# Softmax denominators of a sliding-window attention: from TensorE matmuls to a ones column in V and a VectorE partition shuffle, with TensorE tile modes batched by the scheduler

## The chip, the cores and the metric

One core of a Trainium2 chip. The time is the device time of one execution in microseconds (us). Ratios are computed as the mean time of one kernel's fast runs over that of the other's of the same rounds on the same chip, so they are not quite the ratio of the medians that are quoted beside them. The experiments ran on four occasions, whose medians of the kernel before were 432.86, 433.57, 433.21 and 433.63 us; compare times across occasions by their ratios.

## The reference, cut to what matters

Four layers over x of 2048 tokens by 448 channels, in bf16: attention, gated MLP, attention, gated MLP, each after a layer norm and with a residual. The attention has 16 heads of 28 channels, and every query sees 8 keys at distances 0, 2, ..., 14:

```python
x = x + _A_ref(_layernorm(x, axis=-1), A_wqkv, A_wo)            # layer 0
x = x + _B_ref(_layernorm(x, axis=-1), B_w_gate, B_w_up, B_w_down)  # layer 1
x = x + _A_ref(_layernorm(x, axis=-1), A_wqkv, A_wo)            # layer 2
x = x + _B_ref(_layernorm(x, axis=-1), B_w_gate, B_w_up, B_w_down)  # layer 3
# in _A_ref:  logits = einsum(q, kg) * scale; attn = softmax(logits); o = einsum(attn, vg)
```

## The kernel before

The program is a list of operations with estimated durations, which a list scheduler puts in a fixed order for each engine when the kernel is built; at run time the engines follow that order and wait for each other by semaphores. It works on even and odd tokens separately, so that the dilated window becomes a dense band, in blocks of up to 120 queries (36 blocks in the two attention layers). One block is: 16 score matmuls (TensorE in row tiles, four heads side by side), Exp on ScalarE (ACT), a mask multiply on VectorE (DVE) or GpSimd (POOL), then this, which is where the change is:

```python
def attn_back(li, qb, slot, prio):
    bk = Banks(2)                              # two PSUM banks (PSUM: the memory that TensorE writes; 8 banks)
    for b in range(4):                         # denominators: ones^T E, on 32 rows each
        E.matmul(ps[32*b:32*b+32, bk[1], 0:4*nq], ones32[0:nk, :], E_sb[0:nk, slot, b, 0:4*nq], tile_position=(0, 32*b))
    for h in range(H):                         # attention times V, in column tiles
        b, hc = h % 4, h // 4
        E.matmul(ps[32*b:32*b+32, bk[0], hc*nq:hc*nq+nq], v_sb[0:nk, vs, DH*h:DH*h+32], E_sb[0:nk, slot, b, hc*nq:hc*nq+nq], tile_position=(0, 32*b))
    # ACT: R = exp(-ln(denominator));  DVE: oT = ps * R
    ... (cut)
```

oT then goes through the output projection `wo_g` (operation Y), is added to x, and through the next layer norm. The channel count of 448 is three and a half times 128, so most products end in a "tail" of 64 rows; two tails share the array in 64-row tiles. So TensorE has four modes: full (F), 64-row tiles (R64), 32-row tiles for the scores (R32), 32-column tiles for attention times V (C32). The rule by which the scheduler picks an operation for TensorE was simply: the ready one of the highest priority that gets its banks.

```python
cands.sort()                 # by priority
for *_, op in cands:
    ... (bank checks, cut)
    best = op
    break
```

The softmax here doesn't subtract the row's maximum and nothing guards it: scores larger than these inputs give would overflow.

Of the kernel before, what the change touches and what calls it, by code (L numbers as in the profile page):

```python
# [4 lines left out]
ACT = mybir.ActivationFunctionType  # L5
# [3 lines left out]
D = 448  # L9
# [18 lines left out]
TAILS = True  # L28
PE_T = ("00", "01")
HEAD_LN = 4  # L30
POOL_MASK = 2
POOL_WQK = True
LN0 = (1, 1, 2)
# [18 lines left out]

class Op:
    __slots__ = ("engs", "ins", "est", "deps", "mode", "prio", "acquire", "release", "idx", "eng",
                 "dma", "lat", "after", "start", "end", "promise", "cls")

    def __init__(self, **kw):
        for k in self.__slots__:
# [11 lines left out]
class Sched:  # L70
# [74 lines left out]
    def schedule(self):  # L145
        self.holder = [None] * 8
        self.free_at = [-1e9] * 8
        self.last_rel = [None] * 8
        free = {e: 0.0 for e in self.ENGS}
        order = {e: [] for e in self.ENGS}  # L150
        mode = None
        open_promise = 0
        ndep, users = {}, {}
        pend = {e: [] for e in self.ENGS}
        self.dgroup = {}
        for op in self.ops:
            if op.dma is not None:
                self.dgroup.setdefault((op.dma, op.mode), []).append(op)
        for op in self.ops:
            srcs = set()  # L160
            for k in op.deps:
                src = self.ready[k][0]
                srcs |= {src.idx} if src.dma is None else {o.idx for o in self.dgroup[(src.dma, src.mode)]}
            if op.after is not None:
                srcs.add(op.after.idx)
            ndep[op.idx] = len(srcs)
            for s in srcs:
                users.setdefault(s, []).append(op)
            if not srcs:
                for e in op.engs:  # L170
                    pend[e].append(op)
        left = len(self.ops)
        now = 0.0
        while left:
            moved = False
            b_ready = any(o.acquire is not None and o.acquire.kind == 1 for o in pend["pe"])
            for e in self.ENGS:
                if free[e] > now + 1e-6:
                    continue
                best = None  # L180
                cands = []
                for op in pend[e]:
                    r = self.ready_at(op, e)
                    if r <= now + 1e-6:
                        cands.append((op.prio if e == "pe" or not FIFO else op.cls, r if e != "pe" and FIFO else 0, op.idx, op))
                cands.sort()
                a_wait = False
                for *_, op in cands:
                    if op.acquire is not None:
                        if op.promise > 0 and open_promise:  # L190
                            continue
                        held = [0, 0]
                        for h in self.holder:
                            if h is not None:
                                held[h.kind] += 1
                        kind = op.acquire.kind
                        cap = (A_CAP if b_ready else 8) if kind == 0 else (B_CAP if a_wait else 8)
                        if op.promise >= 0 and held[kind] + op.acquire.n + (op.promise * 2) > cap:
                            continue
                        if self.pick_banks(op.acquire, now) is None:  # L200
                            if kind == 0:
                                a_wait = True
                            continue
                    best = op
                    break
                if best is None:
                    continue
                op = best
                op.eng = e
                for x in op.engs:  # L210
                    pend[x].remove(op)
                if op.acquire is not None:
                    op.acquire.b = self.pick_banks(op.acquire, now)
                    for b in op.acquire.b:
                        self.holder[b] = op.acquire
                        if self.last_rel[b] is not None:
                            op.deps.append(self.last_rel[b])
                open_promise += op.promise
                est = op.est[e]
                if e == "pe":  # L220
                    if mode is not None and op.mode != mode:
                        est += self.SWITCH
                    mode = op.mode
                op.start, op.end = now, now + est
                free[e] = op.end
                order[e].append(op)
                for bk, i in op.release:
                    b = bk.b[i]
                    assert self.holder[b] is bk
                    self.holder[b] = None  # L230
                    self.free_at[b] = op.end + self.TAIL[op.eng]
                    key = ("rel", op.idx, b)
                    self.ready[key] = (op, len(op.ins) - 1)
                    self.last_rel[b] = key
                left -= 1
                moved = True
                for u in users.get(op.idx, ()):
                    ndep[u.idx] -= 1
                    if ndep[u.idx] == 0:
                        for x in u.engs:  # L240
                            pend[x].append(u)
            if moved:
                continue
            nxt = None
            for e in self.ENGS:
                if not pend[e]:
                    continue
                if free[e] > now + 1e-6:
                    c = [free[e]]
                else:  # L250
                    c = [self.ready_at(op, e) for op in pend[e]]
                    c += [f + self.LAT for f in self.free_at]
                c = [t for t in c if t > now + 1e-6]
                if c and (nxt is None or min(c) < nxt):
                    nxt = min(c)
            assert nxt is not None, "stuck"
            now = nxt
        self.order = order
        self.total = max(op.end + op.lat for op in self.ops)
# [77 lines left out]
def build(nc, A_x, A_wqkv, A_wo, B_w_gate, B_w_up, B_w_down, out):  # L337
# [46 lines left out]
    def one(fn, key=None):  # L384
        return [(fn, key)]
# [28 lines left out]
    sc.add("pool", one(lambda E: E.memset(WQK[:].rearrange("p c w (h e) -> p (c w h) e", e=32)[:, :, DH:32], 0.0), "c_wqk0"), 700, prio=-45)  # L414
    memset("pool", xnT[0][:, :, 0:PAD], 0.0, "c_p0", 150)
    memset("pool", xnT[0][:, :, SEG:SEG + PAD], 0.0, "c_p1", 150)
    memset("pool", v_sb[:, :, D:D + 32], 0.0, "c_v", 200)
    memset("pool", qk[:, :, :, 0:PAD], 0.0, "c_p2", 200)
    memset("pool", qk[:, :, :, SEG:SEG + PAD], 0.0, "c_p3", 200)
    memset("pool", MK[:], 1.0, "i_mk0", 300)  # L420
# [174 lines left out]
    def v_group(li, qbs, prio):  # L595
# [31 lines left out]
        s0 = slots[0][0]  # L627
        nk = infos[0][4]
        def fn(E):
            dst = v_sb[0:nk, s0:s0 + n, 0:D]  # L630
            src = ps[0:nk, bk[0]:bk[0] + n, 0:D]
            return E.activation(dst, src, ACT.Copy) if hasattr(E, "activation") else E.tensor_copy(dst, src)  # L632
        sc.add(("act", "dve"), one(fn, [("V", li, q) for q in qbs]), {"act": act_est(n * D), "dve": dve_est(n * D)},
               deps=list(keys) + [p for _, p in slots] + ["c_v"], release=[(bk, 0), (bk, 1)], prio=prio)
# [3 lines left out]
    def attn_front(li, qb, prio):  # L638
# [5 lines left out]
        deps = [("QK", li, j, c) for j in range(jl, jh + 1) for c in range(4)]  # L644
        slot, prev = ring("e", ("AV", li, qb))
        bk = Banks(4, pair=True)
        ins = []
        for h in range(H):
            b, hc = h % 4, h // 4
# [17 lines left out]

    def attn_back(li, qb, slot, prio):
        r, k, t0, nq, nk, tok = qb_info(qb)
        bk = Banks(2)  # L670
        vs = vslot[(li, qb)]
        ins = []
        for b in range(4):
            ins.append((lambda E, b=b: E.matmul(ps[32 * b:32 * b + 32, bk[1], 0:4 * nq], ones32[0:nk, :], E_sb[0:nk, slot, b, 0:4 * nq], start=True, stop=True, tile_position=(0, 32 * b)),  # L674
                        ("Dn", li, qb) if b == 3 else None))
        for h in range(H):
            b, hc = h % 4, h // 4
            ins.append((lambda E, b=b, hc=hc, h=h: E.matmul(ps[32 * b:32 * b + 32, bk[0], hc * nq:hc * nq + nq], v_sb[0:nk, vs, DH * h:DH * h + 32],  # L678
                                                            E_sb[0:nk, slot, b, hc * nq:hc * nq + nq], start=True, stop=True, tile_position=(0, 32 * b)),
                        ("AV", li, qb) if h == H - 1 else None))  # L680
        sc.add("pe", ins, 200.0 + 4 * 54.0, deps=[("E", li, qb, 0), ("E", li, qb, 1), ("V", li, qb), "c_ones"], mode="C32", acquire=bk, prio=prio)
        rs, prev = ring("r", ("N", li, qb))
        sc.add("act", one(lambda E: E.activation(R_sb[:, rs, 0:4 * nq], ps[:, bk[1], 0:4 * nq], ACT.Ln), ("Rl", li, qb)), act_est(4 * nq),  # L683
               deps=[("Dn", li, qb), prev], release=[(bk, 1)], prio=prio)
        sc.add("act", one(lambda E: E.activation(R_sb[:, rs, 0:4 * nq], R_sb[:, rs, 0:4 * nq], ACT.Exp, scale=-1.0), ("R", li, qb)), act_est(4 * nq, False),  # L685
               deps=[("Rl", li, qb)], prio=prio)
        war = [("Y", li - 2, B) for B in range(tok // 128, (tok + nq - 1) // 128 + 1)] if li >= 2 else []
# [190 lines left out]
```

## Time and profile before

432.74 us (median of 3 runs, 432.32 to 433.1). First the page's line of busy times.

```profile
span 431.5 us, 7732 instructions
...
PE 412.2 (96%) x3180; PEld 173.9 (40%) x3220; DVE 244.3 (57%) x482; ACT 221.3 (51%) x350; POOL 24.7 (6%) x38
```

TensorE (PE) is the busiest by far. Whether it is the limit everywhere is read from the windows (busy us of each engine in a stretch, with the number of instructions; the last three columns are granted clock, DMA share and GB/s):

```profile
core 0: us, PE busy (x) PEld busy (x) DVE busy (x) ACT busy (x) POOL busy (x), PEclk, DMA share, GB/s
20.00:40.00 20.00, 17.08 (x208) 7.21 (x208) 11.15 (x23) 17.07 (x25) 6.42 (x3) 1.00 0.74 196
40.00:60.00 20.00, 16.76 (x204) 7.26 (x195) 18.05 (x35) 14.34 (x22) 4.01 (x2) 1.00 0.29 47
...
100.00:150.00 50.00, 49.42 (x438) 20.96 (x435) 32.87 (x71) 30.00 (x47) 0.00 (x0) 1.00 0.17 33
...
250.00:300.00 50.00, 49.58 (x374) 20.72 (x378) 26.97 (x51) 27.04 (x40) 0.00 (x0) 1.00 0.06 12
```

From 100 to 400 us TensorE has about 1% of air (time in which it runs nothing). In the two windows from 20 to 60 us it has 15%, while ACT (17.07 us in the first) or DVE (18.05 us in the second) is as full as it is or fuller. The time up to the first gate matmul of layer 1 is called the head below. Its first record is at 62.52 us; the weight loads around it (62.27, 62.30 and 62.52 us) show that one record is missing, so the head of the kernel before ended some 0.2 us earlier.

"Busy" of TensorE is wide, because matmuls overlap; what a matmul costs is how far it moves the start of the next. That is read from the timeline (start, length, engine, line, shape, how many were merged; an idle gap would stand in brackets):

```profile
104.25 1.49 PE L758 MATMUL ps<-WD,hT 128*128 128x448 bf16 x7
105.67 0.39 PE L650 MATMUL ps<-qk 28*128 28x120 bf16 x16
105.99 1.50 PE L758 MATMUL ps<-WD,hT 128*128 128x448 bf16 x7
...
109.17 0.39 PE L674 MATMUL ps<-E_sb,ones 128*32 128x480 bf16 x4
109.38 0.38 PE L678 MATMUL ps<-E_sb,v_sb 128*32 128x120 bf16 x16
109.69 1.19 PE L551 MATMUL ps<-WV,xnTa 128*72 128x448 bf16 x4
```

Seven matmuls of 448 columns take 105.67 - 104.25 = 1.42 us. Inside a row they follow each other in 189 ns, so 7 x 189 = 1.32 us, and the missing 0.1 us is the step into another tile mode. The four ones matmuls take 109.38 - 109.17 = 0.21 us. Over all records of the trace after 65 us the medians are 189 ns between full matmuls of 448 columns and 283 to 285 ns when a tiled one follows; 216 ns for 512 columns and 309 to 312 ns before a tiled one; 308 ns from the last tail into full mode. A change of mode costs about 94 ns, whichever way it goes.

The groups of the operations in question, from the list by shape (busy us, mean ns of one, idle time before them and what ended it):

```profile
L689 DVE TENSOR_TENSOR oT<-ps,R_sb 128x480 bf16<-128x480 f32 x32 | 20.8, 651 | 12.3 <-ACT R_sb L685 10.6 <-PE ps L551 1.6
...
L674 PE MATMUL ps<-E_sb,ones 128*32 128x480 bf16 x128 | 12.4, 376 | 1.4 <-POOL E_sb L663 1.4
...
L586 DVE CAST qk<-ps 128x1024 bf16<-128x1024 f32 x3 | 3.7, 1222 | 0.9 <-PE ps L524 0.9
```

### The profile page before, as it was taken

What the parts mean: (1) busy time and instruction counts of PE and PEld (TensorE: products, weight loads), DVE (VectorE), ACT (ScalarE), POOL (GpSimd) and SP (SyncE); (2) the same over time, 40 slices, a digit from 0 to 9 for tenths busy, and PEclk for the clock granted to TensorE, in tenths of its full rate; (3) what the DMA queues carried; (4) which work ended last, traced back from release to release, by engine and by line L of the source; (5) the groups of instructions that cost most, each with busy time, mean ns of one, the idle gap of its engine ahead of it and who ended that gap; (6) DMA issues with size and microseconds to landing.
All of it is one profiled execution on the core that took longest, in us unless ns stands there. A gap on an engine that the chain in (4) does not pass through costs nothing.

```text
span 431.5 us, 7732 instructions
## 1 busy us (share of the span) xinstructions
PE 412.2 (96%) x3180; PEld 173.9 (40%) x3220; DVE 244.3 (57%) x482; ACT 221.3 (51%) x350; POOL 24.7 (6%) x38
## 2 busy tenths in 40 slices
PE   6897799999999999999999999999999999999997
PEld 4333334444443345334453334433444344344333
DVE  5746967465896278514887148822876432442332
ACT  4679766756565673347643565346853321321330
POOL 3715210000000000000000000000000000000000
PEclk9999999999999999999999999999999999999999
DMA  8794130100031200200202200010022101001001
GB/s 283 223 277 75 26 50 14 38 0 2 2 74 30 45 2 2 49 2 1 50 2 61 38 2 2 14 38 0 14 59 47 24 11 33 0 2 43 0 2 43
DMA packets 37220, 18.11 MB, mean 42 GB/s; under 512 B 31137, under 2 KB 36273, under 8 KB 37185
## 3 DMA queue, kind: packets, MB, share of 16 engines
q1 hardware_dynamic: 34880, 11.02, 11.7%
q0 software_dynamic: 1152, 5.22, 4.1%
q10 hardware_dynamic: 1152, 1.38, 1.0%
q8 instruction: 25, 0.41, 0.4%
q14 instruction: 11, 0.08, 0.1%
HBM read 8.43 MB, written 1.84 MB: 24 GB/s over the span
## 4 chain that ended last, share of the span: by engine, by line
PE 87%; ACT 5%; issue 4%; DMA 2%; DVE 1%; POOLq 0%; POOL 0%; SPq 0%; DVEq 0%
PE ps L512 47%; PE ps L758 20%; PE ps L524 9%; PE ps L703 5%; ACT E_sb L657 2%; PE ps L674 2%; PE ps L650 2%; DMA x_sb<-in_A_x_dram 2%; PE ps L678 1%; PE ps L551 1%; ACT R_sb L683 1%; ACT qk L586 0%; POOLq L831 0%; POOL E_sb L663 0%; ACT R_sb L685 0%
## 5 line engine op out<-in xcount | busy, mean ns | idle before, releaser
L746 DVE TENSOR_TENSOR hT<-g_sb,ps 128x512 bf16<-128x512 bf16 x112 | 75.9, 685 | 94.2 <-ACT g_sb L743 69.9
L743 ACT ACTIVATE g_sb<-ps 128x512 bf16<-128x512 f32 x112 | 65.7, 598 | 93.0 <-PE ps L524 78.8
L758 PE MATMUL ps<-WD,hT 128*128 128x448 bf16 x448 | 91.0, 353 | 0.0
L512 PE MATMUL ps<-xnTb,WU 128*128 128x512 bf16 x327 | 89.5, 379 | 1.1 <-issue 0.6
L512 PE MATMUL ps<-xnTb,WG 128*128 128x512 bf16 x313 | 86.4, 380 | 2.9 <-issue 1.4
L657 ACT ACTIVATE E_sb<-ps 128x960 bf16<-128x960 f32 (+1 forms) x72 | 63.3, 926 | 29.8 <-PE ps L650 29.8
L708 DVE TENSOR_TENSOR x_sb<-x_sb,ps 128x448 bf16<-128x448 bf16 x64 | 39.2, 613 | 34.0 <-PE ps L758 25.5
L663 DVE TENSOR_TENSOR E_sb<-E_sb,MK 128x960 bf16<-128x960 bf16 (+1 forms) x66 | 41.0, 625 | 29.8 <-ACT E_sb L657 29.4
L758 PEld LDWEIGHTS ps<-WD,hT 128*128 128x128 bf16 x448 | 42.1, 98 | 39.1
L512 PE MATMUL ps<-xnTa,WQK 128*128 128x512 bf16 x184 | 46.6, 390 | 3.0 <-ACT WQK L434 1.6
L512 PEld LDWEIGHTS ps<-xnTb,WU 128*128 128x128 bf16 x336 | 32.1, 98 | 38.4 <-issue 0.6
L512 PEld LDWEIGHTS ps<-xnTb,WG 128*128 128x128 bf16 x336 | 26.4, 97 | 50.2 <-issue 29.2
L473 DVE BATCH_NORM_STATS2 st<-x_sb 128x6 f32<-128x448 bf16 x64 | 39.1, 618 | 4.1 <-DMA x_sb<-in_A_x_dram 3.2
L586 ACT ACTIVATE qk<-ps 128x1024 bf16<-128x1024 f32 x29 | 29.7, 1024 | 20.1 <-PE ps L524 13.8
L524 PE MATMUL ps<-xnTb,WT 64*128 64x512 bf16 x224 | 33.9, 381 | 0.0
L683 ACT ACTIVATE R_sb<-ps 128x480 f32<-128x480 f32 (+1 forms) x36 | 19.7, 550 | 22.0 <-PE ps L674 22.0
L689 DVE TENSOR_TENSOR oT<-ps,R_sb 128x480 bf16<-128x480 f32 (+1 forms) x36 | 22.4, 625 | 14.2 <-ACT R_sb L685 12.4
L703 PE MATMUL ps<-wo_g,oT 128*128 128x448 bf16 x128 | 28.9, 353 | 1.1 <-DVE oT L689 1.0
L512 PEld LDWEIGHTS ps<-xnTa,WQK 128*128 128x128 bf16 x192 | 17.0, 99 | 28.4 <-issue 9.2
L484 DVE TENSOR_SCALAR xn_sb<-x_sb,mv,rstd 128x512 bf16<-128x512 bf16 x64 | 23.5, 426 | 2.8 <-ACT rstd L478 2.7
L512 PE MATMUL ps<-WV,xnTa 128*128 128x448 bf16 x96 | 21.4, 353 | 0.9 <-ACT E_sb L657 0.8
L632 ACT ACTIVATE v_sb<-ps 128x896 bf16<-128x896 f32 (+1 forms) x17 | 14.8, 873 | 13.5 <-PE ps L524 13.1
(55 smaller groups left out, 210.8 us busy)
## 6 DMA issues: line engine op xcount, KB each, us to landing
x_sb<-in_A_x_dram SPq DMA_DIRECT2D x4, 448.0 KB, 7.8
out_dram<-x_sb SPq DMA_DIRECT2D x16, 112.0 KB, 1.7
WD<-in_B_w_down_dram POOLq DMA_DIRECT2D x1, 1568.0 KB, 14.4
WG<-in_B_w_gate_dram POOLq DMA_DIRECT2D x3, 448.0 KB, 5.0
WU<-in_B_w_up_dram POOLq DMA_DIRECT2D x3, 448.0 KB, 7.9
hT<-in_A_wqkv_dram ACTq DMA_DIRECT2D x4, 224.0 KB, 5.1
xnTb<-xn_sb SPq DMA_TRANSPOSE x32, 2.5
WV<-in_A_wqkv_dram ACTq DMA_DIRECT2D x4, 112.0 KB, 6.1
```

The lines of the kernel that those rows point to most:

```text
L473: sc.add("dve", one(lambda E, B=B: E.bn_stats(st6[:, B, :], x_sb[:, B, :]), ("bn", li, B)), 525.0, deps=[("x", li - 1, B)] + ([("xn", li - ...
L512: ins.append((lambda E, u=u, c=c, st=st, sp_=sp_, which=which: E.matmul(u["out"](which), u["lhs"](which, c, 0, 128), u["rhs"](which, c, 0, ...
L524: ins.append((lambda E, u=u, c=c, lo=lo, which=which, opening=opening: E.matmul(u["out"](which), u["lhs"](which, c, lo, lo + 64), u["rhs"] ...
L586: return E.activation(dst, src, ACT.Copy) if hasattr(E, "activation") else E.tensor_copy(dst, src)
L657: return E.activation(E_sb[0:nk, slot, 2 * hp:2 * hp + 2, 0:4 * nq], ps[0:nk, b0:b0 + 2, 0:4 * nq], ACT.Exp, scale=SCALE)
L663: return E.tensor_tensor(e, e, m, ALU.mult)
L683: sc.add("act", one(lambda E: E.activation(R_sb[:, rs, 0:4 * nq], ps[:, bk[1], 0:4 * nq], ACT.Ln), ("Rl", li, qb)), act_est(4 * nq), deps= ...
L703: ins.append((lambda E, hc=hc: E.matmul(ps[:, bk[0], 0:D], oT[:, hc, lo:hi], wo_g[:, hc, :], start=hc == 0, stop=hc == 3), ("Y", li, B) if ...
L708: sc.add("dve", one(lambda E: E.tensor_tensor(x_sb[:, B, :], x_sb[:, B, :], ps[:, bk[0], 0:D], ALU.add), ("x", li, B)), dve_est(D), deps=[ ...
L743: sc.add("act", one(lambda E, gs=gs, bk=bk: E.activation(g_sb[:, gs, :], ps[:, bk[0], :], ACT.Copy), ("G", li, j, fc)), act_est(512), deps ...
L746: sc.add("dve", one(lambda E, gs=gs, bk=bk, fc=fc: E.tensor_tensor(hT[:, fc, hs, :], g_sb[:, gs, :], ps[:, bk[1], :], ALU.mult), ("H", li, ...
L758: ins.append((lambda E, fc=fc, bk=bk, i=i: E.matmul(ps[:, bk[0], 0:D], hT[:, fc, hs, 128 * i:128 * i + 128], WD[:, fc, :], start=fc == 0, ...
```

## The change

Two things. (1) V gets a stride of 32 columns per head instead of 28, and the four spare columns hold ones. The attention matmul is 32 columns wide anyway, so row 28 of each group of 32 PSUM rows now holds the denominator at no extra TensorE work; a DVE shuffle copies that row to all 32 rows, and Ln, Exp and the multiply go on as before. Only the first four blocks (`D_PE = 1`) keep the ones matmuls. (2) When TensorE is in full mode, the scheduler holds tiled operations back until two are ready (`HOLD_N`) or one has waited long enough; once in a tiled mode, it takes all ready tiled operations before it returns.

```diff
-    memset("pool", v_sb[:, :, D:D + 32], 0.0, "c_v", 200)
+    sc.add("pool", one(lambda E: E.memset(v_sb[:]...[:, :, DH:32], 1.0), "c_v"), 400, prio=-40)
@@ scheduler
-                    best = op
-                    break
+                    okay.append(op)
+                    if e != "pe":
+                        break
+                if okay and e == "pe":
+                    nf = [op for op in okay if op.mode != "F"]
+                    ff = [op for op in okay if op.mode == "F"]
+                    if mode not in (None, "F"):
+                        same = [op for op in nf if op.mode == mode]
+                        best = (same or nf or ff)[0]
+                    elif not nf or not ff:
+                        best = okay[0]
+                    else:
+                        over = [now - op.seen >= ((HOLD_BA if op.prio < -5 else HOLD_BB) if b_ready else HOLD_A) for op in nf]
+                        if len(nf) >= HOLD_N or any(over):
+                            best = nf[0]
+                        else:
+                            best = ff[0]
@@ attn_front: an order between blocks
+        if (li > 0 or jh >= S_AFTER) and qb % NQP:
+            deps = deps + [("E", li, qb - 1, 0), ("E", li, qb - 1, 1)]
@@ attn_back
+        by_pe = li == 0 and (tok + nq - 1) // 512 < D_PE
+        bk = Banks(2 if by_pe else 1)
         for b in range(4):
+            if not by_pe:
+                break
             ins.append(... ones matmul ...)
-            ... v_sb[0:nk, vs, DH * h:DH * h + 32] ...
+            ... v_sb[0:nk, vs, 32 * h:32 * h + 32] ...
+            sc.add("dve", one(lambda E: E.stream_shuffle(R_sb[:, rs, 0:4 * nq], ps[:, bk[0], 0:4 * nq], [DH] * 32), ("Rs", li, qb)), dve_est(4 * nq) + 100.0, ...)
+            sc.add("act", one(lambda E: E.activation(R_sb[...], R_sb[...], ACT.Ln), ("Rl", li, qb)), ...)
```

(Cut: constants, the write of V with the new stride, the estimates, most of the lines that these replace, and the old path, which stays for blocks with `by_pe`.)

More of the change, by code (lines that the diff above doesn't have):

```diff
@@ L30 @@
 HEAD_LN = 4
+HOLD_A = 1000.0
+HOLD_BA = 3000.0
+HOLD_BB = 0.0
+HOLD_N = 2
+D_PE = 1
+S_AFTER = 2
 POOL_MASK = 2
@@ L54 @@
     __slots__ = ("engs", "ins", "est", "deps", "mode", "prio", "acquire", "release", "idx", "eng",
-                 "dma", "lat", "after", "start", "end", "promise", "cls")
+                 "dma", "lat", "after", "start", "end", "promise", "cls", "seen")
     def __init__(self, **kw):
@@ L187, in schedule @@
                 a_wait = False
+                okay = []
                 for *_, op in cands:
@@ L203, in schedule @@
                             continue
-                    best = op
-                    break
+                    okay.append(op)
+                    if e != "pe":
+                        break
+                hold = None
+                if okay and e == "pe":
+                    for op in okay:
+                        if op.seen is None:
+                            op.seen = now
+                    nf = [op for op in okay if op.mode != "F"]
[11 more added lines that the diff above has]
+                            best = ff[0]
+                elif okay:
+                    best = okay[0]
                 if best is None:
@@ L416, in build @@
     memset("pool", xnT[0][:, :, SEG:SEG + PAD], 0.0, "c_p1", 150)
-    memset("pool", v_sb[:, :, D:D + 32], 0.0, "c_v", 200)
+    sc.add("pool", one(lambda E: E.memset(v_sb[:].rearrange("p s (h e) -> p (s h) e", e=32)[:, :, DH:32], 1.0), "c_v"), 400, prio=-40)
     memset("pool", qk[:, :, :, 0:PAD], 0.0, "c_p2", 200)
@@ L629, in fn @@
         def fn(E):
-            dst = v_sb[0:nk, s0:s0 + n, 0:D]
-            src = ps[0:nk, bk[0]:bk[0] + n, 0:D]
+            dst = v_sb[0:nk, s0:s0 + n, :].rearrange("p s (h e) -> p s h e", e=32)[:, :, :, 0:DH]
+            src = ps[0:nk, bk[0]:bk[0] + n, 0:D].rearrange("p s (h e) -> p s h e", e=DH)
             return E.activation(dst, src, ACT.Copy) if hasattr(E, "activation") else E.tensor_copy(dst, src)
@@ L669, in attn_back @@
         r, k, t0, nq, nk, tok = qb_info(qb)
-        bk = Banks(2)
+        by_pe = li == 0 and (tok + nq - 1) // 512 < D_PE
+        bk = Banks(2 if by_pe else 1)
         vs = vslot[(li, qb)]
@@ L677, in attn_back @@
             b, hc = h % 4, h // 4
-            ins.append((lambda E, b=b, hc=hc, h=h: E.matmul(ps[32 * b:32 * b + 32, bk[0], hc * nq:hc * nq + nq], v_sb[0:nk, vs, DH * h:DH * h + 32],
+            ins.append((lambda E, b=b, hc=hc, h=h: E.matmul(ps[32 * b:32 * b + 32, bk[0], hc * nq:hc * nq + nq], v_sb[0:nk, vs, 32 * h:32 * h + 32],
                                                             E_sb[0:nk, slot, b, hc * nq:hc * nq + nq], start=True, stop=True, tile_position=(0, 32 * b)),
                         ("AV", li, qb) if h == H - 1 else None))
-        sc.add("pe", ins, 200.0 + 4 * 54.0, deps=[("E", li, qb, 0), ("E", li, qb, 1), ("V", li, qb), "c_ones"], mode="C32", acquire=bk, prio=prio)
+        sc.add("pe", ins, (200.0 if by_pe else 0.0) + 4 * 54.0, deps=[("E", li, qb, 0), ("E", li, qb, 1), ("V", li, qb), "c_ones", "c_v"], mode="C32", acquire=bk, prio=prio)
         rs, prev = ring("r", ("N", li, qb))
-        sc.add("act", one(lambda E: E.activation(R_sb[:, rs, 0:4 * nq], ps[:, bk[1], 0:4 * nq], ACT.Ln), ("Rl", li, qb)), act_est(4 * nq),
-               deps=[("Dn", li, qb), prev], release=[(bk, 1)], prio=prio)
+        if by_pe:
+            sc.add("act", one(lambda E: E.activation(R_sb[:, rs, 0:4 * nq], ps[:, bk[1], 0:4 * nq], ACT.Ln), ("Rl", li, qb)), act_est(4 * nq),
+                   deps=[("Dn", li, qb), prev], release=[(bk, 1)], prio=prio)
+        else:
+            sc.add("dve", one(lambda E: E.stream_shuffle(R_sb[:, rs, 0:4 * nq], ps[:, bk[0], 0:4 * nq], [DH] * 32), ("Rs", li, qb)), dve_est(4 * nq) + 100.0,
+                   deps=[("AV", li, qb), prev], prio=prio)
+            sc.add("act", one(lambda E: E.activation(R_sb[:, rs, 0:4 * nq], R_sb[:, rs, 0:4 * nq], ACT.Ln), ("Rl", li, qb)), act_est(4 * nq, False),
+                   deps=[("Rs", li, qb)], prio=prio)
         sc.add("act", one(lambda E: E.activation(R_sb[:, rs, 0:4 * nq], R_sb[:, rs, 0:4 * nq], ACT.Exp, scale=-1.0), ("R", li, qb)), act_est(4 * nq, False),
```

## The prediction

> **What bounds it.** TensorE. The page: PE 412.2 of 431.5 us busy (96%), DVE 57%, ACT 51%, clock at full throughout. In the timeline its matmuls start back to back. In windows, PE is busy 49.4 to 49.8 of every 50 us from 100 to 400 us. The exception is the head, up to the first gate matmul at 62.5 us: in 20-40 us and 40-60 us PE is busy 17.1 and 16.8 of 20 us, while ACT (17.1) or DVE (18.1) is fuller.
>
> **What the change does, costed from the timeline.**
> 1. Ones matmuls. The four 128x480 ones matmuls of a query block push the next group back 0.21 us (109.17 to 109.38); the short block costs 0.12 us. They stay for the first 4 blocks and go for 32: 28 x 0.213 + 4 x 0.12 = 6.4 us of PE. V columns stay 32 wide, so the ones column is free for PE.
> 2. Tile modes. A WD matmul advances PE 189 ns, but 283 ns when a tiled group follows; 128x512 goes 216 to 312 ns into row tiles, tails 216 to 308 ns out of them, and a direct step between two tiled modes costs the same. So about 94 ns per change. The Trainium skill, "TensorEngine Tiling (Array Packing)", Key Properties, says a mode change drains TensorE; the trace agrees, with 94 ns. By the instruction orders, changes go from 290 to 252: 38 x 94 ns = 3.6 us (head 40 to 44, rest 250 to 208).
> 3. Added to DVE: 32 shuffles of 128x480 f32 from PSUM. The same-size PSUM multiply into oT takes 0.65 us; I estimate 0.6 to 0.65 us each, near 20 us in all (57% to about 63%). ACT keeps its count; Ln only reads SBUF instead of PSUM. The attention tail gets one more hop, about 0.7 us, plus deliberate holding.
>
> **On the critical path.** After the head, all PE savings count: 5.8 us of ones and 42 x 94 ns = 3.9 us of changes; DVE and ACT have slack, so I expect no new PE stalls. In the head the order differs: about 5.0 us of PE work (12+4 QK, 8 output-projection, two AV groups) moves ahead of the first gate matmul and could fill the 6.5 us that PE idles between 33 and 62.5 us. But DVE carries, by a sum of measured durations, about 9 us more before the first hidden multiply, 3 us of it shuffles. So I expect part absorbed: first gate matmul at 65 to 67.5 us.
> Rest before: 431.5 - 62.5 = 369.0; after: 369.0 - 5.8 - 3.9 - 5.0 = 354.3. Plus head 66.5, plus 1.2 (time minus span): 422.0 us, -2.5%.
>
> **Time: 422.0 us, 8 in 10 between 418.0 and 426.5.** Chances: faster over 2% (below 424.1) 0.70; within 2% 0.28; slower 0.02.
>
> **What would show it.** Page: 16 ones matmuls instead of 144; PE busy down by 9 to 11 us; still 96 to 97%; a shuffle group of 32 on DVE at 0.6 to 0.7 us mean; DVE near 63%. Windows from 100 us on: PE still 49.4+ of 50. Advance at mode changes still 94 ns. First gate matmul at 65 to 67.5 us.
>
> **What would make it wrong.** Shuffles much dearer than 0.65 us; the head, DVE-bound, growing beyond 68 us (then within 2%); holding that delays the chain so that PE waits in the rest; or, on the good side, the head's idle fully filled (418 us).

## The result, and the profile after

420.48 us (median of 4 runs, 420.4 to 420.54) against 432.92 us of the kernel before on the same occasion: ratio 0.9714, 95% interval 0.9697 to 0.9731. A later occasion gave 0.9701 for the same kernel. The page:

```profile
span 418.8 us, 7454 instructions
...
PE 400.5 (96%) x3047; PEld 174.3 (42%) x3092; DVE 273.7 (65%) x553; ACT 210.0 (50%) x341; POOL 28.1 (7%) x40
```

The same windows as before:

```profile
20.00:40.00 20.00, 17.08 (x194) 7.07 (x198) 12.61 (x24) 16.23 (x24) 6.42 (x3) 1.00 0.72 196
40.00:60.00 20.00, 17.75 (x250) 7.83 (x246) 18.68 (x43) 18.14 (x29) 9.38 (x5) 1.00 0.16 34
100.00:150.00 50.00, 49.42 (x378) 21.88 (x382) 36.36 (x76) 23.67 (x38) 0.00 (x0) 1.00 0.11 22
250.00:300.00 50.00, 49.26 (x395) 21.43 (x398) 33.80 (x70) 25.60 (x42) 0.00 (x0) 1.00 0.15 29
```

TensorE has as little air after the head as before. Work was taken out of it and the rest moved up. The timeline shows the new batches and blocks without ones matmuls:

```profile
112.48 0.39 PE L680 MATMUL ps<-qk 28*128 28x120 bf16 x16
112.81 0.61 PE L552 MATMUL ps<-xnTb,WT 64*128 64x512 bf16 x4
113.34 0.82 PE L540 MATMUL ps<-xnTb,WG 128*128 128x512 bf16 x3
...
116.04 0.39 PE L711 MATMUL ps<-E_sb,v_sb 128*32 128x120 bf16 x16
116.36 0.60 PE L552 MATMUL ps<-xnTb,WT 64*128 64x512 bf16 x4
116.90 1.19 PE L579 MATMUL ps<-WV,xnTa 128*72 128x448 bf16 x4
```

Scores and tails now stand next to each other, and so do attention and tails: three changes of mode for two groups instead of four. The groups that answer to those shown of before:

```profile
L728 DVE TENSOR_TENSOR oT<-ps,R_sb 128x480 bf16<-128x480 f32 x32 | 20.8, 651 | 8.4 <-ACT R_sb L724 7.9 <-PE ps L552 0.4
L720 DVE STREAM_SHUFFLE R_sb<-ps 128x480 f32<-128x480 f32 x28 | 19.4, 692 | 0.0
...
L614 DVE CAST qk<-ps 128x1024 bf16<-128x1024 f32 x8 | 9.8, 1224 | 6.1 <-PE ps L540 4.9 <-PE ps L552 1.1
...
L720 DVE STREAM_SHUFFLE R_sb<-ps 128x256 f32<-128x256 f32 x4 | 1.8, 440 | 0.0
...
L707 PE MATMUL ps<-E_sb,ones 128*32 128x480 bf16 x16 | 1.5, 375 | 1.3 <-POOL E_sb L693 1.3
```

A shuffle of 480 columns takes 692 ns, one of 256 columns 440 ns, so 1.125 ns per column and 152 ns besides. The Trainium skill, "VectorE: DVE Perf Modes", section "The perf-mode tier table", gives about 2400 ns for 2048 columns and the same speed class whatever the source; the line through our two points would give 2456 ns (an estimate), which agrees. DVE also got five more of the qk evictions (copies of Q and K out of PSUM; 3 to 8, 1.22 us each) and some of V, which ACT lost: which of the two does them is the scheduler's choice. That is why DVE grew by 29.4 us and not by the 21.2 us of shuffles alone.

Now the sum. "PE work" is what TensorE needs if it never waits: every matmul of the instruction order at the advance measured above, plus 94 ns per change of mode of the order. "Head" is the time to the first gate matmul, "rest" the span from there to the end, both from the traces. The experiments' rows are used further down.

| kernel | changes | PE work, head | head | left in head | PE work, rest | rest | left in rest | time, us (ratio to before) |
|---|---|---|---|---|---|---|---|---|
| before | 290 | 43.1 | 62.5 | 19.4 | 360.3 | 369.0 | 8.7 | 432.92 (1) |
| changed | 252 | 47.8 | 65.4 | 17.6 | 346.0 | 353.4 | 7.4 | 420.48 (0.9714) |
| the same, second profile (after_again) | 252 | 47.8 | 64.1 | 16.3 | 346.0 | 354.1 | 8.1 | 420.42 (0.9701) |
| ones_back | 252 | 48.7 | 65.3 | 16.6 | 351.2 | 358.6 | 7.4 | 425.74 (0.9837) |
| unbatch | 293 | 48.6 | 65.6 | 17.0 | 349.1 | 356.9 | 7.8 | 423.89 (0.9788) |
| shuffle_twice | 252 | 47.8 | 67.1 | 19.3 | 346.0 | 359.5 | 13.5 | 427.87 (0.9886) |
| dve_beside | 252 | 47.8 | 68.4 | 20.6 | 346.0 | 355.3 | 9.3 | 425.56 (0.9819) |
| twice_known | 260 | 46.5 | 66.6 | 20.1 | 348.0 | 359.7 | 11.7 | 426.92 (0.9849) |
| shuffle_only | 299 | 46.6 | 66.6 | 20.0 | 351.6 | 360.0 | 8.4 | 428.23 (0.9872) |
| batch_only | 249 | 42.6 | 62.8 | 20.2 | 357.0 | 367.2 | 10.2 | 431.53 (0.9954) |
| batch_tuned | 246 | 45.9 | 64.9 | 19.0 | 353.5 | 361.9 | 8.4 | 429.16 (0.9903) |
| dpe0 | 252 | 43.3 | 67.7 | 24.4 | 349.7 | 357.9 | 8.2 | 426.71 (0.9845) |

"Left in rest" holds a fixed part of some 7 us, which every kernel has: 2.74 us after the last matmul in every trace, and roughly another 4 us of small differences of the estimate (the traces of before and after hold 298 and 260 real changes, because a lone 64-row V tail changes the mode without the scheduler's knowledge). What clearly exceeds 8 us there is waiting. The PE work is good to about 0.4 us: at 0.213 us for a group of ones matmuls (0.12 us for a short one) and 94 ns per change, before and changed differ by 6.4 + 3.6 = 10.0 us, where the table has 9.6 us.

The two profiles of the changed kernel show how far the split can be trusted. Their heads differ by 1.3 us, and the difference arises at the start, where the same three QK matmuls took 1.46 us in the first profile and 0.82 us in the second:

```profile
16.06 1.46 PE L540 MATMUL ps<-xnTa,WQK 128*128 128x512 bf16 x3
```

```profile
15.63 0.82 PE L540 MATMUL ps<-xnTa,WQK 128*128 128x512 bf16 x3
```

TensorE starts at half speed in every trace (last section), and how long that lasts differs from run to run. The second group of QK tails begins at 23.37 us in the first profile and at 22.08 us in the second; from there to the first gate matmul both take 42.01 us. Where a small difference of heads matters, it is counted from these tails: 39.4 us before (39.2 with the missing record), 42.0 changed, 42.6 ones_back, 42.5 unbatch, 44.0 shuffle_twice and dpe0, 45.0 dve_beside. The rests of the two profiles differ by 0.7 us; the second has one wait of 0.6 us for a transposed input that the first has not.

So of the 12.7 us of span, 9.6 us are PE work (403.4 to 393.8 us), 1.8 us are less idle time in the head, and 1.3 us are less left over in the rest. (The last two are differences of sums, not waits that I could point to one by one. Counted from the tails the head grew by 2.6 us (2.8 with the missing record) with 4.7 us more PE work, in both profiles, so some 2 us filled there are well founded. The 1.3 us of the rest are hardly more than the scatter of 0.7 us and the 0.4 us of the PE work.)

### The profile page after: what moved, and what is told of

It is laid out like the page before. It is cut to its first block, busy times and chain, and to the rows that moved or that the text cites. A ratio compares the mean times of both kernels' runs of the same rounds, so it can differ in the third digit from the quotient of the medians.

```text
span 418.8 us, 7454 instructions
## 1 busy us (share of the span) xinstructions
PE 400.5 (96%) x3047; PEld 174.3 (42%) x3092; DVE 273.7 (65%) x553; ACT 210.0 (50%) x341; POOL 28.1 (7%) x40
## 4 chain that ended last, share of the span: by engine, by line
PE 88%; DVE 5%; ACT 3%; DMA 2%; issue 1%
PE ps L540 47%; PE ps L797 20%; PE ps L552 10%; PE ps L742 5%; PE ps L711 2%; PE ps L680 2%; ACT E_sb L687 1%; DVE qk L614 1%; PE ps L579 1%; DMA x_sb<-in_A_x_dram 1%; DVE st L501 1%; DVE oT L728 1%; DMA xnTb<-xn_sb 1%; DVE E_sb L693 1%; DVE x_sb L747 1%
## 5 line engine op out<-in xcount | busy, mean ns | idle before, releaser
L785 DVE TENSOR_TENSOR hT<-g_sb,ps 128x512 bf16<-128x512 bf16 x112 | 74.5, 684 | 32.5 <-ACT g_sb L782 25.2
L782 ACT ACTIVATE g_sb<-ps 128x512 bf16<-128x512 f32 x112 | 64.7, 599 | 58.2 <-PE ps L552 48.2
L797 PE MATMUL ps<-WD,hT 128*128 128x448 bf16 x448 | 89.4, 353 | 0.0
L797 PEld LDWEIGHTS ps<-WD,hT 128*128 128x128 bf16 x448 | 43.0, 98 | 41.0 <-issue 0.4
L540 PEld LDWEIGHTS ps<-xnTb,WG 128*128 128x128 bf16 x336 | 27.7, 98 | 48.2 <-issue 24.0
L614 ACT ACTIVATE qk<-ps 128x1024 bf16<-128x1024 f32 x24 | 24.5, 1022 | 42.2 <-PE ps L552 37.1
L660 ACT ACTIVATE v_sb<-ps 128x896 bf16<-128x896 f32 (+1 forms) x13 | 11.4, 888 | 26.2 <-PE ps L552 25.4
L722 ACT ACTIVATE R_sb<-R_sb 128x480 f32<-128x480 f32 (+1 forms) x32 | 18.4, 575 | 11.5 <-DVE R_sb L720 11.5
L512 DVE TENSOR_SCALAR xn_sb<-x_sb,mv,rstd 128x512 bf16<-128x512 bf16 x64 | 22.6, 405 | 2.4 <-ACT rstd L506 2.4
```

Of the source, the lines that this page charges most:

```text
L540: ins.append((lambda E, u=u, c=c, st=st, sp_=sp_, which=which: E.matmul(u["out"](which), u["lhs"](which, c, 0, 128), u["rhs"](which, c, 0, ...
L614: return E.activation(dst, src, ACT.Copy) if hasattr(E, "activation") else E.tensor_copy(dst, src)
L782: sc.add("act", one(lambda E, gs=gs, bk=bk: E.activation(g_sb[:, gs, :], ps[:, bk[0], :], ACT.Copy), ("G", li, j, fc)), act_est(512), deps ...
L785: sc.add("dve", one(lambda E, gs=gs, bk=bk, fc=fc: E.tensor_tensor(hT[:, fc, hs, :], g_sb[:, gs, :], ps[:, bk[1], :], ALU.mult), ("H", li, ...
L797: ins.append((lambda E, fc=fc, bk=bk, i=i: E.matmul(ps[:, bk[0], 0:D], hT[:, fc, hs, 128 * i:128 * i + 128], WD[:, fc, :], start=fc == 0, ...
```

## The experiments

Theory: after the head TensorE is the limit, so time follows PE work; in the head DVE and ACT are, so PE work there is nearly free and DVE work is dear. Rivals: the gain came from the new order or the freed PSUM bank, with ones matmuls and mode changes hidden; or one of the two parts did it all; or the shuffles take part of the gain away.

### ones_back: the ones matmuls returned, the order kept

```diff
+        for b in range(4):
+            if by_pe:
+                break
+            ins.append((lambda E, b=b: E.matmul(ps[32*b:32*b+32, bk[0], 0:4*nq], ones32[0:nk, :], E_sb[0:nk, slot, b, 0:4*nq], ...), None))
         for h in range(H):      # overwrites the same bank
```

> The changed kernel with its instruction order untouched, and the 128 ones matmuls of the 32 shuffled blocks put back on TensorE; what they write is overwritten by the attention matmuls of the same bank, so the result is right and the shuffles stay. Theory (after the head TensorE is the limit, so every removed matmul is time): 28 x 0.213 + 4 x 0.12 = 6.4 us more PE work, of it 5.3 us after the first gate matmul and 0.97 us in the head, where idle may swallow it: 425.7 to 426.9 us. Rival (the gain came from the new order and from the PSUM bank that each block no longer holds, the ones matmuls being hidden): under 422.5 us.

Measured 425.74 us (0.9837). The timeline shows the returned group costing the same 0.21 us as before:

```profile
106.31 0.39 PE L712 MATMUL ps<-E_sb,ones 128*32 128x480 bf16 x4
106.52 0.38 PE L715 MATMUL ps<-E_sb,v_sb 128*32 128x120 bf16 x16
```

The table splits it: 5.2 us more PE work in the rest, 5.2 us more time there (353.4 to 358.6 us; 4.4 us against the second profile); 0.9 us more PE work in the head, no more time there (65.4 to 65.3 us). But the last is the luck of the start: counted from the QK tails the head grew by 0.55 us (42.01 to 42.56). So after the head a removed matmul is time, about one for one; in the head about half of it is.

### unbatch: the mode changes returned, the order kept

```diff
+    if op.mode != "F" and last_mode not in (None, "F", op.mode) and op.acquire is not None:
+        E.matmul(ps[:, b, 0:1], warm[:, 0:128], warm[:, 0:1], start=True, stop=True)   # b: the bank that op is about to overwrite
```

> The changed kernel with its order untouched; where one tiled group follows directly on a group of another tile mode (41 places) a 128-row matmul of one column is put between, so that the array goes back to full mode and out again: one change of mode more at each place, as in the kernel before. Theory (a change costs 94 ns and lies on the critical path): 41 x 0.094 = 3.9 us plus 41 tiny matmuls, by an estimate 0.03 to 0.06 us each (the 120-column ones advance 54 ns): 425.0 to 427.0 us. Rival (changes of mode are free or hidden; batching acts only by order): 420.5 to 422.5 us.

Measured 423.89 us (0.9788), under the expected range. The timeline shows one such place:

```profile
113.32 0.39 PE L685 MATMUL ps<-qk 28*128 28x120 bf16 x16
113.64 0.18 PE L866 MATMUL ps<-warm 128*128 128x1 bf16 x1
113.75 0.61 PE L557 MATMUL ps<-xnTb,WT 64*128 64x512 bf16 x4
```

From the start of the one-column matmul to the tails it is 0.11 us, and 107 to 111 ns at 40 of the 41 places: the 94 ns of a change and 16 ns for the matmul, not the 30 to 60 ns that I had estimated. 32 places lie after the head: 32 x 0.110 = 3.5 us (the table, which prices the tiny matmul lower, has 3.1), and the rest grew by 3.5 us (353.4 to 356.9 us; 2.8 us against the second profile). The nine in the head, 1.0 us of PE work, added 0.5 us counted from the QK tails. So a change of mode is on the critical path at its full price; the expectation missed because it took too much for the tiny matmul and counted the head in full.

### shuffle_twice and dve_beside: is the added DVE work free?

shuffle_twice repeats each shuffle, the second waiting for the first:

```diff
-            sc.add("dve", one(shuffle, ("Rs", li, qb)), ...)
+            sc.add("dve", [(shuffle, None), (shuffle, ("Rs", li, qb))], ...)      # same estimate, so the same order
```

> The changed kernel with its order untouched and each of the 32 shuffles done twice, the second after the first has ended. Adds 28 x 0.69 + 4 x 0.44 = 21 us of DVE work (65% to about 69 or 70% busy). Theory (DVE has slack after the head and is close to the limit in it): rest unchanged within 0.5 us, first gate matmul later by 0.5 to 3.5 us, so 421.0 to 424.5 us. Rival A (shuffles are entirely free): 420.3 to 420.8. Rival B (the shuffle sits in the chain that TensorE waits for everywhere, so part of the gain is lost to it): over 426 us.

Measured 427.87 us (0.9886): rival B's range, and far more than I expected. The head grew by 1.7 us (2.0 us from the QK tails), the rest by 6.1 us. The table of waits of TensorE (who waited for whom, us in total, times, longest) has a new first line, where the changed kernel has 0.4 us; the second is from the table for all engines and is that of the weight loads:

```profile
PE ps L745 <- DVE oT L731: 4.1, 8, 1.2
```

```profile
PEld ps L745 <- DVE oT L731: 12.1, 20, 1.5
```

The output projection waits for oT, the last link of the chain attention, shuffle, Ln, Exp, multiply. After the head 2.2 of the 4.1 us remain, and 8.5 of the 12.1 us of the weight loads; the matmuls' listed waits there come to 3.1 us in all, so part of the 6.1 us is not pinned to single waits. Two causes remained: DVE has no room for 21 us more, or the chain has no room for 0.7 us more. dve_beside keeps the chain as it was and gives DVE the work beside it, right after each shuffle:

```diff
+            sc.dummy[sh.idx] = lambda E: E.bn_stats(du_sb[:], ps[:, bk[0], 0:4 * nq])   # emitted after the shuffle has signalled
```

> The changed kernel with its order untouched; right after each of the 32 shuffles DVE reads the same PSUM bank once more (a statistics operation of about 0.65 us, its result unused), so that DVE gets about as much work as in the doubled shuffle (near 20 us), but the wait of Ln for the shuffle is not longer. Chain theory (the doubled shuffle cost 7.4 us because the chain from attention to the output projection got 0.7 us longer, not because DVE was full): 420.5 to 423.5 us, with TensorE waiting for oT under 1.5 us. Rival (DVE has no room for 20 us): 425.5 us or more.

Measured 425.56 us (0.9819), outside my range and in the rival's. DVE got what was meant, as this group of the list by shape shows, and the wait for oT is smaller but there (2.0 us of it in the head, 0.7 us after it):

```profile
L728 DVE BATCH_NORM_STATS2 du_sb<-ps 128x6 f32<-128x480 f32 x28 | 18.1, 648 | 0.0
```

```profile
PE ps L752 <- DVE oT L738: 2.6, 4, 1.6
```

The split tells more than the total. In the head dve_beside cost 3.0 us (65.4 to 68.4 us, and the same from the QK tails), more than the doubled shuffle did; in the rest it cost 1.9 us against 6.1 us (1.2 against 5.3 us when the second profile is the measure). So each cause holds in its own place. The head has no room on DVE. In the rest DVE had room for about 17 us of additional work at a loss of 1.9 us, while the same amount inside the chain cost three times that. What the rest lacks is slack in the chain.

### twice_known: the same long chain, but known to the scheduler

```diff
-            ... ("Rs", li, qb))], dve_est(4 * nq) + 100.0, ...
+            ... ("Rs", li, qb))], 2 * dve_est(4 * nq) + 240.0, ...
```

> The doubled shuffle again (427.87 us; TensorE then waited for oT in the output projection), but with the scheduler told that it takes twice as long, so that it may put other work before the projection. PE work by its order 394.5 us, 0.75 us over the changed kernel. Theory (the loss came from a static order that was made for the short shuffle; DVE itself has the room): 422 to 425.5 us. Rival (the DVE work or the longer chain is a real limit at 70% busy): 427 us or more.

Measured 426.92 us (425.3 to 428.07; 0.9849): 1 us better than the ignorant order, worse than I expected, and too scattered to settle more. The profile is of the slowest of the four runs. In it the wait of the projection for oT is gone from TensorE's table of waits; another has come, once, at the transposed input of the MLP, which is the end of the next, longer chain (projection, residual, layer norm, transpose). The timeline there:

```profile
349.31 0.40 PE L713 MATMUL ps<-E_sb,v_sb 128*32 128x120 bf16 x16
351.74 1.35 PE L542 MATMUL ps<-xnTb,WG 128*128 128x512 bf16 x3 [2.04 <-DMA xnTb<-xn_sb]
352.88 1.48 PE L542 MATMUL ps<-xnTb,WU 128*128 128x512 bf16 x3
```

So in this run the scheduler, told of the longer chain, moved the wait and did not remove it. Whether the order alone was at fault stays open: the median lies between the two ranges, and the fastest run (425.3 us) is inside the theory's. Three matmuls that take 0.81 us elsewhere take 1.48 us just after that wait, at half the granted clock (last section).

### shuffle_only, batch_only, batch_tuned: each part alone

```diff
 shuffle_only:   best = okay[0] (the old rule); S_AFTER = 99
 batch_only:     by_pe = True (ones matmuls in all 36 blocks)
 batch_tuned:    by_pe = True; HOLD_A = 0; HOLD_BA = 8000
```

> The ones column and the shuffle with the scheduler's old rule (highest priority first, no holding, no extra order between blocks). By its order 299 modelled changes of mode against 252, ones matmuls as in the changed kernel, so 47 x 0.094 = 4.4 us more PE work than the changed kernel and 5.3 us less than the kernel before. Theory (time follows PE work): 424.0 to 427.0 us. Rival (the batching contributes nothing): 420 to 421.5 us.

Measured 428.23 us, ratio 0.9872: 1.3% under the kernel before, about the 5.2 us of PE work that it saves against it. It missed the range because I had counted from the changed kernel, which also has less idle time.

> The batching scheduler with ones matmuls in all 36 blocks and no shuffle. By its order 249 modelled changes of mode against 290 before: 41 x 0.094 = 3.9 us less PE work than before. Theory (time follows PE work): 427.5 to 430.0 us. Rival (the ones column is the whole gain, batching delays chains and gives its saving back): 431.5 to 433.5 us. Other rival (batching is the whole gain): 420 to 422 us.

Measured 431.53 us, ratio 0.9954: half of what its PE work promises. The rest held 10.2 us over its PE work instead of 8.7, and TensorE had new waits after the head, 1.4 us for masks (the longest 1.0 us) and 0.5 us for hT. The waits for oT in the table lie in the head, the longest at 48.4 us:

```profile
PE ps L742 <- DVE oT L728: 1.7, 2, 1.3
...
PE ps L707 <- DVE E_sb L693: 1.4, 2, 1.0
```

> Batching alone, ones matmuls in all blocks, with holding times chosen again for it (HOLD_A 0, HOLD_BA 8000). PE work by its order 399.3 us, 4.1 us under the kernel before and 0.3 us under the untuned form, which gained only 2.0 us and showed 1.85 us of new TensorE waits after the head. Theory (those waits came from holding times fitted to the other kernel): 428.5 to 430.5 us. Rival (batching loses half its saving whenever the shuffle is not there): 431 to 432.5 us.

Measured 429.16 us, ratio 0.9903, in the range: with holding times chosen for it, batching alone gives 1.0%, about the 4.0 us of its PE work. The lost half was a matter of the holding times; one was shortened (HOLD_A, 1 us to 0) and one lengthened (HOLD_BA, 3 to 8 us), and which of the two did it was not tested.

So neither part is the whole. Alone they give 1.3% and 1.0%, together 2.9% (3.0% on the second occasion). The PE work of the two adds up (5.2 + 4.0 = 9.2 of 9.6 us). The 3 us over it are time that the combined order leaves idle less (table), about 2 us of it in the head. I did not isolate which property of the order does that; the PSUM bank that each shuffled block no longer holds is one candidate, untested by itself.

### dpe0: shuffles in the first four blocks too

```diff
-D_PE = 1
+D_PE = 0
```

> The changed kernel with the shuffle in all 36 blocks, none of them with ones matmuls. PE work falls by a further 0.8 us, DVE gets 4 more shuffles (2.8 us) in the head, and the scheduler makes another order (252 modelled changes, as before it). Theory (the head is limited by DVE and ACT, so relief of PE there buys nothing): 421 to 425 us, slower than the changed kernel. Rival (PE work decides in the head too): 419.5 to 420.0 us.

Measured 426.71 us (0.9845), over 5 us slower than the changed kernel, though its PE work is 0.8 us less: the direction of the theory, but beyond its range. The head grew to 67.7 us with 4.5 us less PE work in it. DVE is full where TensorE waits, and in the profiled run the waits were followed by a spell of half clock, as the window and the timeline show:

```profile
40.00:60.00 20.00, 16.68 (x198) 6.72 (x198) 19.05 (x37) 15.48 (x24) 10.30 (x5) 0.83 0.16 33
```

```profile
42.83 0.59 PE L711 MATMUL ps<-E_sb,v_sb 128*32 128x120 bf16 x16 [1.55 <-DVE x_sb L747]
43.35 2.42 PE L540 MATMUL ps<-WV,xnTa 128*128 128x448 bf16 x6
```

Six V matmuls took 2.42 us where they take 1.31 us elsewhere. But the other three runs, whose granted clock over the span was 0.992 and not 0.98, needed 426.5 to 426.88 us against 427.4 us of this one. So that spell explains less than 1 us; most of the loss is idle time of TensorE in the head (24.4 us left there instead of 17.6), and the PE work not done there follows in the rest (349.7 instead of 346.0 us). The scheduler also made another order, so the full DVE is not the only thing that changed. That the change keeps ones matmuls for just the first four blocks fits this: there TensorE has time and DVE has none.

### tail_tuned, after_again, tail_again: a better version?

The lone 64-row V tail, which sits between full matmuls, was made an operation of tile mode that can be batched, and holding times were set again:

```diff
-        for i, c in enumerate((0, 1, 2, 3)):      # c == 2 has 64 rows, all one operation of mode "F"
+        for i, c in enumerate((0, 1, 3)):         # mode "F"
+        sc.add("pe", one(tail c == 2), ..., mode="R64", after=op)
-HOLD_BA = 3000.0; HOLD_BB = 0.0; S_AFTER = 2; A_CAP = 4
+HOLD_BA = 4000.0; HOLD_BB = 1000.0; S_AFTER = 3; A_CAP = 6
```

> An attempt at a better version: the single V groups, whose 64-row matmul stands between full matmuls and changes the mode twice without the scheduler knowing (the traces show 298 and 260 changes where its model has 290 and 252), get that matmul as a tile-mode operation of its own that can be batched; holding times set again (HOLD_BA 4000, HOLD_BB 1000, S_AFTER 3, A_CAP 6). 250 changes, all known, against 260: 10 x 0.094 = 0.9 us. Theory: 419.0 to 420.2 us. Rival (the head or new waits eat it): 420.3 us or more.

Measured 419.79 us (0.9686), which looked like a gain. Since 0.3% between occasions is within their scatter, both were run again side by side:

> The changed kernel once more, as the measure for the others on this chip: ratio to before 0.971 to 0.973.

> The better version of the last call once more, beside the changed kernel on the same chip: 0.9 us less by 10 changes of mode, so 0.5 to 1.5 us below it (ratio to before lower by 0.001 to 0.0035).

The changed kernel gave 420.42 us (420.01 to 420.84) and the other 420.16 us (419.01 to 420.85), both at a ratio of 0.9701. The expected 0.5 us or more is not there: the same, within the scatter. No version beat the changed kernel.

## Why the prediction was right

422.0 us were predicted, 418.0 to 426.5 us as the range; 420.48 us came. Step by step:

- "After the head, all PE savings count": shown. ones_back and unbatch put 5.2 and 3.5 us back into the rest and got 5.2 and 3.5 us of time (4.4 and 2.8 us against the second profile of the changed kernel).
- Price of the ones matmuls (6.4 us, 5.8 us of it in the rest): right, 0.21 us per block in both traces. What of it counts is what lies in the rest of the new order, and that is 5.2 us.
- "About 94 ns per change", 38 changes: right, and measured by itself (110 ns with the tiny matmul). The Trainium skill's sentence that a mode change drains TensorE ("TensorEngine Tiling (Array Packing)", Key Properties) fits: the price is paid at the change alone, and inside a group the matmuls on different tiles of one mode start 3 to 4 ns apart.
- The rest: 354.3 us predicted, 353.4 us measured. The head: 66.5 us predicted, 65.4 us measured, in the stated 65 to 67.5 us, which was in part luck: in the second profile, with a shorter slow start, it was 64.1 us. By the first profile that is together 2.0 us too long, and 0.5 us too short for the time outside the span (1.2 us taken, 1.7 us measured), which makes the 1.5 us of difference. The mis-sized term is idle time: about 3 us less of it came with the new order, of which I had expected only 0.7 us in the head (4.0 us of growth for 4.7 us of PE work) and nothing in the rest. In the head 1.8 us came; what came in the rest is near the scatter. PE busy fell by 11.7 us, not 9 to 11, and one window after the head shows 49.26 us, under the stated 49.4.
- "Head DVE-bound": shown by dpe0 and by dve_beside, where DVE work placed there cost 3 us of head.
- Shuffles at 0.6 to 0.65 us: a little low, 0.69 us for the long ones. DVE at "about 63%": low, 65%, because the scheduler moved evictions from ACT to DVE; "ACT keeps its count" was wrong for the same reason (350 to 341).
- "DVE and ACT have slack, so I expect no new PE stalls": right in its result (TensorE waited 0.4 us for oT in the whole changed kernel), but for a weaker reason than I gave. DVE has room after the head; the chain does not. Had the shuffle taken twice its time, 6.1 us of the rest would have been lost, as shuffle_twice showed. My estimate of the shuffle mattered more than the prediction allowed for.

## What to carry to other kernels

When one engine is the limit, price a change by how far each removed instruction moves the start of the next, and count it only where that engine has no air; here the same matmul was worth about 0.21 us after 65 us and about half of that before. In a tiled TensorE kernel count the changes of tile mode in the instruction order: at 94 ns each, 290 of them were 27 us of 432. Work moved to an engine with idle time is not free if it lands inside a chain whose end the busy engine needs at a fixed place: ask for the slack of the chain, not only for the share of busy time.

## What the Trainium skill lacked or had wrong

- "TensorEngine Tiling (Array Packing)", Key Properties, says that a mode change drains TensorE and gives no price: 94 ns of start-to-start time here, into and out of full mode and between two tiled modes alike; 110 ns with a one-column matmul between two tiled groups.
- "TensorE: Matmul & The Clock Gate", Part 1, puts the return to half clock after an idle window of about 3.4 us, and its table of goals allows gaps of up to about 3 us. Shorter waits sufficed: in twice_known a single wait of 2.04 us, with TensorE busy before and after it, was followed by a granted clock of 0.50, as the windows show (the column before the last two):

```profile
349.00:351.00 2.00, 0.70 (x19) 0.23 (x16) 1.95 (x7) 0.00 (x0) 0.00 (x0) 1.00 0.59 120
351.00:353.00 2.00, 1.26 (x4) 0.52 (x5) 0.70 (x2) 1.20 (x2) 0.00 (x0) 0.72 0.41 130
353.00:355.00 2.00, 2.00 (x22) 0.65 (x22) 0.54 (x1) 0.06 (x1) 0.00 (x0) 0.50 0.00 0
```

  TensorE was busy for all 9 us from 340 to 349 us. In the profiled run of dpe0 several waits of 1.6 us and less were also followed by 0.50, but a wait of 1.97 us in batch_tuned (to 51.09 us) was followed by 1.00, and three matmuls after it took the usual 0.81 us. So the length of one wait does not decide it; what does was not tested.
- "VectorE: DVE Perf Modes" has the shuffle at 2048 columns alone. For short ones the fixed part matters: 152 ns + 1.125 ns per column from PSUM in f32, the line through two sizes (692 ns at 480 columns, 440 ns at 256).
- "TensorE: Matmul & The Clock Gate", Part 1, warns that the trace's events of the clock gate have been seen to be unreliable, but has no case like this one: a recorded clock of 1.00 where TensorE ran at half speed. In the first 20 us the record of the changed kernel has 0.74 and that of the kernel before 1.00, but the same first six QK matmuls took 2.74 us in both, and in all fourteen traces, where six take 1.46 us later. The prediction's "clock at full throughout" came from this record. The kernel before:

```profile
12.48 2.74 PE L512 MATMUL ps<-xnTa,WQK 128*128 128x512 bf16 x6 [1.62 <-ACT WQK L434]
...
71.01 1.46 PE L512 MATMUL ps<-xnTa,WQK 128*128 128x512 bf16 x6
```

  The changed kernel:

```profile
12.41 2.74 PE L540 MATMUL ps<-xnTa,WQK 128*128 128x512 bf16 x6 [1.62 <-ACT WQK L462]
```

  So mean clocks are no measure of lost time here: runs of the changed kernel with a mean of 0.988 and of 1.0 over the span took 420.45 to 420.54 and 420.4 to 420.5 us.
